# Block-sorted attention with a gated FFN: value mixing of batches 1 to 3 by pairs of 64-row matmuls

## The chip, the cores and the metric

The kernel runs on one core of a Trainium2 chip. The metric is the device time of one execution in microseconds (us). Before the change it was 250.72 us, the median of 5 runs (250.2 to 250.99).

## What is computed

Four batches of eight heads, each a sequence of 768 positions with 64 channels. Each head's sequence is cut into 8 blocks of 96 positions. A small 8x8 matrix P per head is normalised five times over rows and columns. K and V are then mixed block by block with P (each sorted block is a weighted sum of the 8 blocks), and each query block attends to its own sorted block. The result goes through a gated FFN (512 to 1536 to 512).

```
k_sorted = einsum('bhij,bhjcd->bhicd', P, k_b)
v_sorted = einsum('bhij,bhjcd->bhicd', P, v_b)
scores   = scale * q_b @ k_sb^T            # per block of 96
attn     = softmax(scores)
x        = (attn @ v_sb), heads side by side   # 3072 x 512
out      = (silu(x @ w_gate) * (x @ w_val)) @ w_out
```

## The kernel before, in words

**Layout.** There are 64 pairs of (head, block) per batch. V of a batch is loaded with these pairs on 64 partitions: batch 0 and batch 2 on partitions 0 to 63 (`lowr`), batch 1 and batch 3 on 64 to 127 (`highr`). `copy_v` then turns it, for each partition, from (position, channel) order into (channel, position) order in the tile `vch`, so that the 96 positions of one channel lie together. There is one `vch`; batches 0, 1 and the pair of 2 and 3 use it in turn.

**Mixing of the values.** For one channel, a matmul takes the 64 partitions' 96 positions as its stationary operand and a 64x64 matrix `rmix` (P of the eight heads along the diagonal) as its moving operand. Batch 0 does this with 64 rows. For batch 1 all 128 rows of `vch` are multiplied with a `rmix[1]` whose lower 64 rows are zero (`v_chunk`, 64 moving columns). For batches 2 and 3, `rmix["p"]` is 128 x 128, block diagonal over the two batches, so that one matmul per channel gives both (`v_pair_chunk`, 128 moving columns). A chunk fills a PSUM tile of two banks, tag "a" or "b", which ScalarE or VectorE drains into the tile `vt` (`drain`, 96x1024). Batch 1 has four chunks of 16 channels, the pair eight chunks of 8.

**Other matmuls.** `kq_chunk` mixes K and moves Q (output tile tkq); each pair of its matmuls goes to the two column halves of the array. `scores` (qk) runs 64-row matmuls of 96 columns in pairs on the two row halves. `av` applies the softmax. `gate` (g_ps), `value` (v_ps) and `outp` (o_ps) are the FFN, in eight stages of 384 positions.

**Order.** TensorE's and GpSimd's instruction orders are written out by hand. `merge` takes the FFN matmuls of a stage as its main list and slips the attention's pieces in at given positions; batch 1's value chunks lie in stage 1 and the pair's in stage 3. VectorE's and ScalarE's orders are by hand in the start-up and otherwise left to a scheduler. The GpSimd queue issues the loads and the larger casts and does most of `copy_v`: for batch 1 four copies of 64x1536, then the loads `kp` and V of batches 2 and 3 (which reuse V's tile), the casts of Q, and the copies of the pair.

**Weights.** P reaches the 64-partition layout by small matmuls; `w_sb` keeps what the later batches need, in a ScalarE copy for each half of the partitions, and `mix_of` multiplies it with a mask into `rmix` on VectorE.

Of the kernel before, what the change touches and what calls it, by code (L numbers as in the profile page):

```python
# [10 lines left out]
BF16 = mybir.dt.bfloat16  # L11
# [6 lines left out]
def kernel(  # L18
# [11 lines left out]
    nc = tc.nc  # L30

    B, H, S, D = q.shape
    NB = sort_net.shape[-1]
    C = S // NB
# [9 lines left out]
    R = H * NB  # L44
# [9 lines left out]
    const = ctx.enter_context(tc.tile_pool(name="const", bufs=1))  # L54
# [20 lines left out]
    vch = const.tile([128, D * C + 32], BF16)  # L75
    nc.vector.memset(vch[:, D * C:], 0.0)
    vch3 = vch[:, 0:D * C].rearrange("p (d c) -> p d c", c=C)
# [36 lines left out]
        load_w(wg_sb, wg_dram, lo, hi)  # L114
        load_w(wv_sb, wv_dram, lo, hi)

    def copy_v(eng, pair, rows, s, n=4, d0=0, d1=D):
        cs = slice(s * (C // n), (s + 1) * (C // n))
        dst = vch3[rows, d0:d1, cs]
        src = v_tiles[pair][rows, cs, d0:d1]  # L120
        if eng is nc.scalar:
            eng.copy(dst, src.transpose([0, 2, 1]))
        else:
            eng.tensor_copy(dst, src.transpose([0, 2, 1]))  # L124

    ident = const.tile([128, 128], BF16)
    lowr, highr = slice(0, R), slice(R, 2 * R)
# [23 lines left out]
    load_q(1, 0, C)  # L151
    nc.gpsimd.dma_start(out=wo_sb, in_=wo_dram)

    rmix = {b: const.tile([128, 2, H, NB], BF16, name=f"rmix{b}") for b in (0, 1, "p")}
    for t in rmix.values():
        nc.vector.memset(t, 0.0)
# [3 lines left out]
    def vt_tile(pair):  # L160
        if pair not in vts:
            t = vtp.tile([C, 2, H * NB, D + 1], BF16, name=f"vt{pair}", tag="vt")
            nc.vector.memset(t[:, :, :, D:D + 1].rearrange("p u n e -> p (u n) e"), 1.0)
            vts[pair] = t
        return vts[pair]
# [10 lines left out]
    def pair_tile(name, tag):  # L176
        return psum.tile([128, 1024], FP32, name=name, tag=tag)

    def bank_tile(name, tag="gen"):
        return psum.tile([128, 512], FP32, name=name, tag=tag, bufs=3 if tag == "gen" else 1)  # L180
# [28 lines left out]
    def drain(eng, dst, src):  # L209
        if eng == "v":  # L210
            nc.vector.tensor_copy(dst, src)  # L211
        else:
            nc.scalar.copy(dst, src)  # L213
# [10 lines left out]
    def chunk_tile(name, n, tag):  # L224
        return pair_tile(name, tag) if n == 2 else bank_tile(name, tag)
# [10 lines left out]
        drain(eng, dst[:, :, at:at + n], tp.transpose([0, 2, 1]))  # L236

    def v_chunk(b, at, n, eng, tag):
        rows = slice(0, 128) if b % 2 else lowr
        dst = vt_tile(b // 2)[:, b % 2]  # L240
        mix = rmix[b][rows, 0].rearrange("p a b -> p (a b)")
        tp = chunk_tile("tv", n // 8, tag).rearrange("p (l n) -> p l n", n=H * NB)
        for ld in range(n):
            col = (at + ld) * C
            nc.tensor.matmul(tp[:, ld, :], lhsT=vch[rows, col:col + 128], rhs=mix,  # L245
                             start=True, stop=True)
        drain(eng, dst[:, :, at:at + n], tp[0:C].transpose([0, 2, 1]))

    def v_pair_chunk(pair, at, n, eng, tag):
        dst = vt_tile(pair).rearrange("p u n e -> p (u n) e")  # L250
        mix = rmix["p"].rearrange("p u a b -> p (u a b)")
        tp = chunk_tile("tv", n // 4, tag).rearrange("p (l n) -> p l n", n=2 * H * NB)
        for ld in range(n):
            col = (at + ld) * C
            nc.tensor.matmul(tp[:, ld, :], lhsT=vch[:, col:col + 128], rhs=mix,  # L255
                             start=True, stop=True)
        drain(eng, dst[:, :, at:at + n], tp[0:C].transpose([0, 2, 1]))

    es, sts, xts = {}, {}, {}
    ecount = [0]  # L260
# [21 lines left out]
    def exps(b, u, wide, pss):  # L282
        n = ecount[0] % 8
        ecount[0] += 2
        if wide is None:
            for two in range(2):
                nc.scalar.activation(e_all[:, n + two, 0:4 * C], pss[two][0:C, 0:4 * C], AF.Exp, scale=scale)
        else:
            nc.scalar.activation(e_all[:, n:n + 2, 0:4 * C], wide[0:C, :, 0:4 * C], AF.Exp, scale=scale)  # L289
        es[(b, u)] = [e_all[:, n, :], e_all[:, n + 1, :]]  # L290

    def qk(b, u, tag="b"):
        exps(b, u, *scores(b, u, tag))
# [29 lines left out]
    def xtr(b, u):  # L323
        half, g = divmod(u, H2)
        if g == 0:
            xts[(b, half)] = xtp.tile([128, H2, TW], BF16, name=f"xt{b}_{half}", tag="xt")
        x_ps = xt_tile("x", 1)[:, 0]
        x_to(x_ps, b, u)
        return xts[(b, half)][:, g, :], x_ps.rearrange("p a b -> p (a b)")
# [83 lines left out]
    def fill(tile, n):  # L413
        for _ in range(n):
            nc.tensor.matmul(tile, lhsT=warm_sb[:, 0:128], rhs=warm_sb, start=True, stop=True)  # L415
# [7 lines left out]
    for it, n in ((1, 3), (2, 4), (3, 4), (4, 4)):  # L423
        nc.tensor.matmul(idle_ps[0:NB, 0:NB], lhsT=rowreds[it][:, :, 0], rhs=rowreds[it][:, :, 0],
                         start=True, stop=True)
        fill(idle_ps, n)

    def weights(half):
        w_ps = bank_tile(f"w_ps{half}")[:, 0:NB * B * H].rearrange("p (i b h) -> p i b h", b=B, h=H)
        for i in range(NB):  # L430
            nc.tensor.matmul(w_ps[half * R:(half + 1) * R, i].rearrange("p b h -> p (b h)"),
                             lhsT=p_bf[:, i].rearrange("p a b -> p (a b)"),
                             rhs=ident[0:BH, 0:BH], start=True, stop=True)
        return w_ps

    def mix_of(dst, b, w):
        lo = (b % 2) * R
        nc.vector.tensor_tensor(dst, mask[lo:lo + R].unsqueeze(2).to_broadcast([R, H, NB]),
                                w[lo:lo + R].transpose([0, 2, 1]), op=ALU.mult)

    w_lo = weights(0)
    mix_of(rmix[0][lowr, 0], 0, w_lo[:, :, 0])
    w_hi = weights(1)
    w_sb = const.tile([128, NB, 2, H], FP32)
    nc.scalar.copy(w_sb[lowr, :, 1], w_lo[lowr, :, 2])
    nc.scalar.copy(w_sb[highr], w_hi[highr].rearrange("p i (pair u) h -> p i pair u h", u=2)[:, :, :, 1])
    fill(idle_ps, 1)
    v_chunk(0, 0, 8, "v", "gen")
# [15 lines left out]
    for b in range(1, B):  # L464
        rows = highr if b % 2 else lowr
        mix_of(rmix["p"][rows, b % 2] if b > 1 else rmix[1][rows, 0], b, w_sb[:, :, b // 2])
    fill(idle_ps, 4)
    qk(0, 0, "a")
    qk(0, 1, "b")
# [48 lines left out]
    def units(b, us, ats):  # L518
        us = list(us)
        todo = []  # L520
        for n, at in enumerate(ats):
            u, u2 = us[2 * n:2 * n + 2]
            held = []
            todo.append((at, lambda u=u, u2=u2, held=held: (qk(b, u, "b"), held.append(scores(b, u2, "a")))))
            todo.append((at + 1.3, lambda u2=u2, held=held: exps(b, u2, *held[0])))
            for w, tag, t in ((u, "b", 1.9), (u2, "a", 3.6)):
                if b == 0 or b == 1 and u < H2:
                    todo.append((at + t, lambda w=w, tag=tag: av(b, w, tag)))
                    todo.append((at + t + 3.1, lambda w=w: drain("v", *xtr(b, w))))
                else:  # L530
                    todo.append((at + t, lambda w=w, tag=tag: (av(b, w, tag), x_dma(b, w))))
        return todo

    def kqs(b, ats):
        return [(at, lambda n=n: (kq_chunk(b, n * 32, 16, "v", "b"), kq_chunk(b, n * 32 + 16, 16, "s", "a")))
                for n, at in enumerate(ats)]

    def vs(f, size, ats):
        return [(at, lambda m=m: f(1, m * size, size, "sv"[m % 2], "ba"[m % 2])) for m, at in enumerate(ats)]

    def merge(main, side):
        done, k = 0.0, 0
        side = sorted(side, key=lambda t: t[0])
        for c, f in main:
            f()
            done += c
            while k < len(side) and side[k][0] <= done:
                side[k][1]()
                k += 1
        while k < len(side):  # L550
            side[k][1]()
            k += 1

    def ffn(n):
        todo = []
        for m in range(NFC):
            if n > 0 or m > 1:
                todo.append((0.65, lambda m=m: gate(n, m)))
            if n > 0 or m > 0:
                todo.append((0.65, lambda m=m: value(n, m)))  # L560
            ends = (6, 9, 11) if n == 1 else (3, 7, 11)
            if n > 0 and m in ends:
                for part in range(3):
                    todo.append((0.87, lambda t3=ends.index(m), part=part: outp(n - 1, t3, part)))
        return todo

    for s in range(4):
        copy_v(nc.gpsimd, 0, highr, s)
    load_k_pair()
    load_v(2, 0, C)  # L570
    load_v(3, 0, C)
# [1 line left out]
    q_cast(3)  # L573
    both = slice(0, 128)
    merge(ffn(0), units(0, range(4, 8), (0.0, 5.6)))
    merge(ffn(1), vs(v_chunk, 16, (3.2, 3.9, 4.7, 5.5)) + kqs(1, (6.2, 8.2, 10.3)) + units(1, range(4), (11.3, 15.8)))
    for s in range(4):
        copy_v(nc.gpsimd, 1, both, s)
    nc.vector.memset(kqt_tile("p")[:, 2 * GI * C:], 0.0)
# [42 lines left out]
```

The softmax here doesn't subtract the row's maximum and nothing guards it: scores larger than these inputs give would overflow.

## Time and profile before

| | |
|---|---|
| median of 5 runs | 250.72 us |
| the profiled execution, its own time | 250.2 us |
| its span in the profile | 248.2 us |
| PE busy | 239.9 us (97%) |
| DVE, ACT, POOL busy | 157.7, 110.2, 52.6 us |
| batch 1's value matmuls (L245, 128 rows) | 64, in 4 blocks from 47.63 us |
| the pair's value matmuls (L255) | 64, in 8 blocks from 107.75 us |
| score matmuls (L276) | 256, 64 rows |

PE is TensorE's matmuls and PEld its weight loads, DVE VectorE, ACT ScalarE, POOL GpSimd. A matmul's duration in the profile is a latency of about 200 ns; matmuls overlap, so the cost of a block is read from the start of one block to the start of the next. A timeline line gives the start and the length from the first start to the last end. In the chain of waits, pieces are put end to end and so show what each adds. A shape such as 64*128 64x96 is rows*columns of the array that are used and the moving operand.

### The profile page before, as it was taken

Reading aid. Unit: us, or ns where it says so; the run is one execution under the profiler, and the core shown is the slowest. Engines: PE = TensorE matmul, PEld = TensorE weight load, DVE = VectorE, ACT = ScalarE, POOL = GpSimd, SP = SyncE. Lnnn points to the kernel's source line nnn. Section 1 sums busy time; section 2 is a strip of 40 time slices with the busy share of each in tenths; the row PEclk is TensorE's granted clock in tenths of the full one; section 3 lists DMA queues with packets and bytes.
Section 4 is the critical chain, followed back from the end, with each engine's and each line's share of the span. In section 5 each row is a group of like instructions: output and inputs, shape, how many; then the busy total and the mean of one; then the engine's idle time right before and its main releaser. Section 6 shows DMA issues by size and latency. Waiting matters only on the chain.

```text
span 248.2 us, 6062 instructions
## 1 busy us (share of the span) xinstructions
PE 239.9 (97%) x2572; PEld 142.8 (58%) x2572; DVE 157.7 (64%) x332; ACT 110.2 (44%) x187; POOL 52.6 (21%) x47
## 2 busy tenths in 40 slices
PE   7799999999999999999999999999999999999995
PEld 5376566666555556666655655565555555555543
DVE  6777689887555775857657647755764585446700
ACT  2977543453544444455642552354244334232311
POOL 7938449980059200000000000000000000000000
PEclk9999999999999999999999999999999999999999
DMA  5949999999999388110122121112111111100122
GB/s 100 209 84 161 214 192 220 199 223 217 220 171 189 71 186 149 43 42 3 42 51 57 51 68 32 44 45 74 26 52 42 38 56 56 45 18 25 45 81 89
DMA packets 39530, 24.38 MB, mean 98 GB/s; under 512 B 27728, under 2 KB 35664, under 8 KB 38992
## 3 DMA queue, kind: packets, MB, share of 16 engines
q0 software_dynamic: 21328, 14.16, 39.0%
q1 hardware_dynamic: 18176, 9.84, 14.3%
q8 instruction: 20, 0.33, 0.6%
q14 instruction: 6, 0.05, 0.1%
HBM read 28.32 MB, written 7.86 MB: 146 GB/s over the span
## 4 chain that ended last, share of the span: by engine, by line
PE 88%; DVE 6%; ACT 3%; issue 2%; DVEq 0%; ACTq 0%
PE v_ps L372 24%; PE g_ps L354 23%; PE o_ps L389 23%; PE tkq L233 4%; PE av_ps L303 3%; PE qk L276 3%; PE idle_ps L415 2%; PE tv L245 2%; PE tv L255 1%; DVE gs_sb L364 1%; PE o_ps L405 1%; DVE st L309 1%; PE x_ps L320 1%; DVE h L377 1%; ACT e_all L289 1%
## 5 line engine op out<-in xcount | busy, mean ns | idle before, releaser
L364 DVE SCALAR_TENSOR_TENSOR gs_sb<-th_sb,g_ps 128x384 bf16<-128x384 bf16 x96 | 52.8, 550 | 53.8 <-ACT th_sb L362 51.2
L372 PE MATMUL v_ps<-xt,wv_sb 128*128 128x384 bf16 x380 | 77.3, 326 | 0.3
L354 PE MATMUL g_ps<-xt,wg_sb 128*128 128x384 bf16 x376 | 76.5, 325 | 0.0
L362 ACT ACTIVATE th_sb<-g_ps 128x384 bf16<-128x384 f32 x96 | 47.1, 490 | 57.7 <-PE g_ps L354 55.2
L389 PE MATMUL o_ps<-wo_sb,h 128*128 128x512 bf16 x276 | 64.3, 379 | 0.0
L377 DVE SCALAR_TENSOR_TENSOR h<-v_ps,gs_sb 128x384 bf16<-128x384 f32 x96 | 53.3, 556 | 6.4
L372 PEld LDWEIGHTS <-wv_sb 128*128 128x128 bf16 x380 | 35.6, 97 | 23.9 <-issue 1.4
L354 PEld LDWEIGHTS <-wg_sb 128*128 128x128 bf16 x376 | 34.5, 97 | 22.9 <-issue 0.2
L389 PEld LDWEIGHTS <-h 128*128 128x128 bf16 x276 | 26.3, 98 | 28.3
L394 ACT COPY o_sb<-o_ps 128x512 f32<-128x512 f32 x23 | 13.5, 585 | 49.1 <-PE o_ps L389 49.1
L124 POOL COPY vch<-v 64x1536 bf16<-64x1536 bf16 (+2 forms) x11 | 28.7, 2643 | 19.6 <-DMA v<-in_v_dram 19.6
L289 ACT ACTIVATE e_all<-qk 96x768 bf16<-96x768 f32 x30 | 22.6, 802 | 7.7 <-PE qk L276 7.6
L309 DVE TENSOR_TENSOR st<-av_ps,r_sb 96x512 bf16<-96x512 f32 x32 | 21.7, 679 | 0.2
L303 PEld LDWEIGHTS <-e_all 96*128 96x128 bf16 x256 | 12.2, 98 | 5.0 <-ACT e_all L289 0.8
L303 PE MATMUL av_ps<-vt,e_all 96*128 96x65 bf16 x256 | 13.5, 194 | 0.0
L307 DVE RECIPROCAL r_sb<-av_ps 96x8 f32<-96x8 f32 x32 | 6.4, 199 | 8.6 <-PE av_ps L303 8.6
L213 ACT CAST vt<-tv 96x1024 bf16<-96x1024 f32 (+1 forms) x9 | 9.2, 1031 | 3.8 <-PE tv L255 2.6
L211 DVE CAST vt<-tv 96x1024 bf16<-96x1024 f32 (+1 forms) x9 | 9.8, 1100 | 1.1 <-PE tv L245 1.1
L211 DVE CAST kqt<-tkq 128x1024 bf16<-128x1024 f32 (+1 forms) x7 | 7.5, 1068 | 2.6 <-PE tkq L233 2.5
L213 ACT CAST kqt<-tkq 128x1024 bf16<-128x1024 f32 (+1 forms) x7 | 6.0, 894 | 6.5 <-PE tkq L233 6.5
L233 PE MATMUL tkq<-rmix,kq 128*64 128x64 bf16 x384 | 7.8, 197 | 0.5 <-issue 0.5
L233 PEld LDWEIGHTS <-kq 128*64 128x64 bf16 x384 | 6.8, 112 | 2.4 <-issue 2.1
(74 smaller groups left out, 131.9 us busy)
## 6 DMA issues: line engine op xcount, KB each, us to landing
out_dram<-o_sb SPq DMA_DIRECT2D x23, 256.0 KB, 2.0
v<-in_v_dram POOLq DMA_DIRECT2D x3, 768.0 KB, 18.6
kq<-in_q_dram POOLq DMA_DIRECT2D x2, 768.0 KB, 13.5
wg_sb<-in_moe_w_gate_dram POOLq DMA_DIRECT2D x6, 256.0 KB, 8.6
wv_sb<-in_moe_w_val_dram POOLq DMA_DIRECT2D x6, 256.0 KB, 9.6
wo_sb<-in_moe_w_out_dram POOLq DMA_DIRECT2D x1, 1536.0 KB, 24.3
kp<-in_k_dram POOLq DMA_DIRECT2D x2, 768.0 KB, 14.0
q_scr<-in_q_dram POOLq DMA_DIRECT2D x2, 768.0 KB, 28.8
```

Of the source, the lines that this page charges most:

```text
L124: eng.tensor_copy(dst, src.transpose([0, 2, 1]))
L211: nc.vector.tensor_copy(dst, src)
L233: nc.tensor.matmul(tp[two * D:(two + 1) * D, lc, :], lhsT=kq_tiles[b][:, at + lc, :], rhs=rm[:, two], start=True, stop=True)
L289: nc.scalar.activation(e_all[:, n:n + 2, 0:4 * C], wide[0:C, :, 0:4 * C], AF.Exp, scale=scale)
L303: nc.tensor.matmul(o[:, two, i4, :], lhsT=e[:, i4 * C:i4 * C + 128], rhs=vt[:, 2 * g + two, half * 4 + i4, :], start=True, stop=True)
L309: nc.vector.tensor_tensor(st.rearrange("p i two d -> p two i d"), o[0:C, :, :, 0:D], r_sb.to_broadcast([C, 2, 4, D]), op=ALU.mult)
L354: nc.tensor.matmul(g_ps, lhsT=wg_sb[:, kc, ts(m, 128)], rhs=xt[:, kc, :], start=(kc == 0), stop=(kc == NKC - 1))
L362: nc.scalar.activation(th_sb, g_ps, AF.Tanh, scale=0.5)
L364: nc.vector.scalar_tensor_tensor(gs_sb, th_sb, 1.0, g_ps, op0=ALU.add, op1=ALU.mult)
L372: nc.tensor.matmul(v_ps, lhsT=wv_sb[:, kc, ts(m, 128)], rhs=xt[:, kc, :], start=(kc == 0), stop=(kc == NKC - 1))
L377: nc.vector.scalar_tensor_tensor(h_tiles[n][:, m, :], v_ps, 0.5, gs_tiles.pop(m), op0=ALU.mult, op1=ALU.mult)
L389: nc.tensor.matmul(o_ps, lhsT=h_w[:, m, ts(t3, 128)], rhs=wo_sb[:, m, :], start=(m == 0), stop=(m == NFC - 1))
```

## The change

Values of batches 1 to 3 are mixed by 64-row matmuls of 64 columns, two for each step of the loop, one on each row half of the array and each into its own PSUM bank (`v_rows_chunk`). For the pair, the two are batch 2 and batch 3 of the same channel. For batch 1, whose V lies on the upper partitions alone, channels 0 to 31 are copied to the lower partitions and channels 32 to 63 to the upper ones; one matmul takes channel d and the other channel d + 32. GpSimd's copies for this are eight of 64x768 instead of four of 64x1536, and four of them write to other partitions than they read. A copy of batch 1's mixing matrix for the lower rows (`vmix`) is made from a part of `w_sb` that a widened ScalarE copy fills. Chunk counts, drains per chunk and their places in the order stay.

```diff
-    def copy_v(eng, pair, rows, s, n=4, d0=0, d1=D):
+    def copy_v(eng, pair, rows, s, n=4, d0=0, d1=D, to=None):
...
-        dst = vch3[rows, d0:d1, cs]
+        dst = vch3[rows if to is None else to, d0:d1, cs]
...
+    vmix = const.tile([R, H, NB], BF16)
...
+    def v_rows_chunk(mixes, dst, at, step, eng, tag):
+        n = 512 // (H * NB)
+        tp = pair_tile("tv", tag).rearrange("p (w l n) -> p w l n", w=2, n=H * NB)
+        for ld in range(n):
+            for w, rows in enumerate((lowr, highr)):
+                col = (w * step + at + ld) * C
+                nc.tensor.matmul(tp[:, w, ld, :], lhsT=vch[rows, col:col + 128], rhs=mixes[w],
+                                 start=True, stop=True)
+        drain(eng, dst[:, :, :, at:at + n], tp[0:C].transpose([0, 1, 3, 2]))
+
+    def v_one_chunk(b, at, n, eng, tag):
+        dst = vt_tile(b // 2)[:, b % 2, :, 0:D].rearrange("p n (w d) -> p w n d", w=2)
+        mixes = [vmix.rearrange("p a b -> p (a b)"), rmix[b][highr, 0].rearrange("p a b -> p (a b)")]
+        v_rows_chunk(mixes, dst, at // 2, D // 2, eng, tag)
+
     def v_pair_chunk(pair, at, n, eng, tag):
-        dst = vt_tile(pair).rearrange("p u n e -> p (u n) e")
-        mix = rmix["p"].rearrange("p u a b -> p (u a b)")
-        tp = chunk_tile("tv", n // 4, tag).rearrange("p (l n) -> p l n", n=2 * H * NB)
-        for ld in range(n):
-            col = (at + ld) * C
-            nc.tensor.matmul(tp[:, ld, :], lhsT=vch[:, col:col + 128], rhs=mix,
-                             start=True, stop=True)
-        drain(eng, dst[:, :, at:at + n], tp[0:C].transpose([0, 2, 1]))
+        mixes = [rmix["p"][rows, u].rearrange("p a b -> p (a b)") for u, rows in enumerate((lowr, highr))]
+        v_rows_chunk(mixes, vt_tile(pair), at, 0, eng, tag)
...
-    nc.scalar.copy(w_sb[lowr, :, 1], w_lo[lowr, :, 2])
+    nc.scalar.copy(w_sb[lowr], w_lo[lowr, :, 1:3])
...
+    mix_of(vmix, 0, w_sb[:, :, 0])
...
     for s in range(4):
-        copy_v(nc.gpsimd, 0, highr, s)
+        copy_v(nc.gpsimd, 0, highr, s, d0=D // 2)
+        copy_v(nc.gpsimd, 0, highr, s, d1=D // 2, to=lowr)
...
-    merge(ffn(1), vs(v_chunk, 16, (3.2, 3.9, 4.7, 5.5)) + kqs(1, (6.2, 8.2, 10.3)) + ...
+    merge(ffn(1), vs(v_one_chunk, 16, (3.2, 3.9, 4.7, 5.5)) + kqs(1, (6.2, 8.2, 10.3)) + ...
```

More of the change, by code (lines that the diff above doesn't have):

```diff
@@ L238, in v_chunk @@
     def v_chunk(b, at, n, eng, tag):
-        rows = slice(0, 128) if b % 2 else lowr
         dst = vt_tile(b // 2)[:, b % 2]
-        mix = rmix[b][rows, 0].rearrange("p a b -> p (a b)")
+        mix = rmix[b][lowr, 0].rearrange("p a b -> p (a b)")
         tp = chunk_tile("tv", n // 8, tag).rearrange("p (l n) -> p l n", n=H * NB)
@@ L244, in v_chunk @@
             col = (at + ld) * C
-            nc.tensor.matmul(tp[:, ld, :], lhsT=vch[rows, col:col + 128], rhs=mix,
+            nc.tensor.matmul(tp[:, ld, :], lhsT=vch[lowr, col:col + 128], rhs=mix,
                              start=True, stop=True)
         drain(eng, dst[:, :, at:at + n], tp[0:C].transpose([0, 2, 1]))
-    def v_pair_chunk(pair, at, n, eng, tag):
-        dst = vt_tile(pair).rearrange("p u n e -> p (u n) e")
-        mix = rmix["p"].rearrange("p u a b -> p (u a b)")
-        tp = chunk_tile("tv", n // 4, tag).rearrange("p (l n) -> p l n", n=2 * H * NB)
-        for ld in range(n):
-            col = (at + ld) * C
-            nc.tensor.matmul(tp[:, ld, :], lhsT=vch[:, col:col + 128], rhs=mix,
-                             start=True, stop=True)
-        drain(eng, dst[:, :, at:at + n], tp[0:C].transpose([0, 2, 1]))
+    def v_rows_chunk(mixes, dst, at, step, eng, tag):
[11 more added lines that the diff above has]
+        v_rows_chunk(mixes, dst, at // 2, D // 2, eng, tag)
+    def v_pair_chunk(pair, at, n, eng, tag):
+        mixes = [rmix["p"][rows, u].rearrange("p a b -> p (a b)") for u, rows in enumerate((lowr, highr))]
+        v_rows_chunk(mixes, vt_tile(pair), at, 0, eng, tag)
     es, sts, xts = {}, {}, {}
@@ L575 @@
     merge(ffn(0), units(0, range(4, 8), (0.0, 5.6)))
-    merge(ffn(1), vs(v_chunk, 16, (3.2, 3.9, 4.7, 5.5)) + kqs(1, (6.2, 8.2, 10.3)) + units(1, range(4), (11.3, 15.8)))
+    merge(ffn(1), vs(v_one_chunk, 16, (3.2, 3.9, 4.7, 5.5)) + kqs(1, (6.2, 8.2, 10.3)) + units(1, range(4), (11.3, 15.8)))
     for s in range(4):
```

## The prediction

> **What bounds the kernel now.** I read the page first: the engines' busy shares, then the chain that ended last.
>
> ```profile
> PE 239.9 (97%) x2572; PEld 142.8 (58%) x2572; DVE 157.7 (64%) x332; ACT 110.2 (44%) x187; POOL 52.6 (21%) x47
> PE 88%; DVE 6%; ACT 3%; issue 2%; DVEq 0%; ACTq 0%
> ```
>
> TensorE is busy 97% of the span and is 88% of the chain. So a nanosecond taken from or added to its stream between 27 us and the end moves the end, unless it is swallowed by a wait of PE. Next, the groups of instructions with shapes kept apart: the two matmul groups that the change rewrites, and the scores, which already run as 64-row pairs.
>
> ```profile
> L276 PE MATMUL qk<-kqt 64*128 64x96 bf16 x128 | 4.4, 204 | 0.7 <-DVE st L309 0.6
> L255 PE MATMUL tv<-rmixp,vch 128*128 128x128 bf16 x64 | 4.9, 219 | 0.0
> L245 PE MATMUL tv<-rmix,vch 128*128 128x64 bf16 x64 | 2.5, 193 | 0.0
> ```
>
> The means (193 to 219 ns) are latencies; what counts is the distance from start to start. Third, the chain in order of time, 47 to 55 us, with start, length and count of each piece:
>
> ```profile
> 47.14 0.65 PE g_ps L354 x4
> 47.79 0.47 PE tv L245 x16
> 48.26 0.65 PE v_ps L372 x4
> ...
> 52.91 0.62 PE tkq L233 x32
> 53.53 0.04 issue
> 53.57 0.70 PE tkq L233 x32
> ```
>
> A block of 16 batch-1 matmuls costs the chain 0.47 us. The first half of the tkq block takes 0.62, though a whole undisturbed block (56.44) takes 1.13: some 0.2 us is a wait in its middle. Fourth, the timelines of POOL, DVE and PE:
>
> ```profile
> 36.16 11.22 POOL L124 COPY vch<-v 64x1536 bf16<-64x1536 bf16 x4 [2.84 <-DMA v<-in_v_dram]
> ```
> ```profile
> 52.29 1.22 DVE L211 CAST vt<-tv 96x1024 bf16<-96x1024 f32 x1 [0.48 <-PE tv L245]
> ```
> ```profile
> 47.63 0.63 PE L245 MATMUL tv<-rmix,vch 128*128 128x64 bf16 x16
> ...
> 83.99 1.03 PE L389 MATMUL o_ps<-wo_sb,h 128*128 128x512 bf16 x4
> 84.95 0.51 PE L276 MATMUL qk<-kqt 64*128 64x96 bf16 x16
> 85.40 0.39 PE L389 MATMUL o_ps<-wo_sb,h 128*128 128x512 bf16 x1
> ```
>
> POOL ends its copies of batch 1 at 36.16 + 11.22 = 47.38 us, and PE reads them from 47.63: 0.25 us of room, the tightest place of the change. The last DVE drain of batch 1 starts when its matmuls end (DVE had idled 0.48 us for them) and ends at 52.29 + 1.22 = 53.51; tkq's second half continues at 53.57. That drain is the wait in the tkq block.
>
> **What the Trainium skill says.** TensorEngine Tiling (Array Packing), Tiling Modes: "Changing tiling mode (not just tile) drains the TensorE". The trace agrees. Four o_ps matmuls from 83.99 stream until 84.85 (4 x 215.8 ns start to start), qk starts 0.096 us later and o_ps returns at 85.40: 0.54 us for 8 pairs whose streaming is 8 x 42.5 = 0.34. TensorE: Matmul & The Clock Gate, Part 3 "The mechanism", has matmuls on different row groups overlap, about 4 ns apart; single starts of qk show 3 to 4 ns in a pair. GPSIMD Engine Reference, Instruction dispatch, describes a fixed software cost per POOL instruction; the trace agrees (below). I found no price there for a POOL copy whose output lies on other partitions.
>
> **The change part by part.**
>
> 1. *Batch 1, four blocks.* Now 16 matmuls of 64 columns at 29.2 ns (single starts) = 0.467 us. After: 8 pairs. From the qk blocks in FFN work: 96 ns to enter the mode; first pair 52 ns (50 plus 3 in the tkq block, also of 64 columns); and from the last start to FFN's next 135 ns, of which 42.5 is its own streaming, so 92 ns to leave. A pair of 64 columns I take at 29.2 ns: qk's pairs keep the distance of one unpaired matmul of their width (96/2.4 + 2.5 = 42.5), and one of 64 columns, weight load included, shows 29.2. Block: 96 + 52 + 6 x 29.2 + 3 + 29.2 + 92 = 448 ns, so -18 each, four times: -0.07 us. Bounds for the pair distance: 31.8 (tkq's column pairs) and 42.5 (64 columns no faster than 96), giving blocks of 464 and 529 ns.
>
> 2. *Batches 2 and 3, eight blocks.* Now 8 matmuls of 128 columns at 55.8 ns = 0.447 us. After, the same 448 ns: +0.01 us in all. The saved half of the streaming goes into two mode changes. With both bounds, all twelve blocks are worth -0.06 (taken), +0.13, or +0.91 us. There are 64 more matmuls and loads, none early enough to touch the start-up; a qk block of 32 such instructions shows no gap inside.
>
> 3. *The wait in the tkq block.* From the start of its slot, batch 1's last block now finishes at 437 + 193 = 630 ns (last start plus latency), after at 96 + 230 + 193 = 519. DVE is idle then, so the drain ends 0.11 us sooner in the slot, while PE arrives only 0.02 sooner: -0.09 us. Bounds: -0.09 and 0.
>
> 4. *POOL's copies.* Four copies of 64x1536 become eight of 64x768, half written to the other 64 partitions. Single POOL copies: 1536 elements 2.84 us, the 64x288 one 0.66, so 1.75 ns an element and 0.155 fixed: 1.50 us for 768. Consecutive starts overlap by 0.05: 1.446. End: 36.16 + 7 x 1.446 + 1.50 = 47.78. Four of the eight carry a semaphore wait that is long satisfied (for start-up's TensorE, ScalarE and POOL work on vch); at start-up a copy with such a wait came 0.04 later than one without: +0.16, so 47.94. PE's first load waits for it. A DVE result reached a waiting PE matmul after 0.055 us, so PE starts at about 48.00 instead of 47.63 + 0.096 = 47.72: +0.27 us. PE is in order, so the whole FFN stream stands behind that load. Bounds: 0, if the fixed part is nearly nothing (end near 47.2); +0.4, if it is the 0.183 us of the one-element copy (landed) and waits cost more. The crossing of partitions has no row; its bounds are none and a doubling, in the rivals. Below nothing: excluded, since PE doesn't wait for POOL now.
>
> 5. *Behind those copies on POOL*: two kp loads, two v loads, two q casts, 0.56 us later. The last four copies begin at 71.18 behind the v loads and end at 82.4, and PE reads them at 107.75: 25 us of cover. kp is read at 93.08; the q transposes on SP come no earlier, and SP's order is unchanged. Zero; were the cover gone, 0.56.
>
> 6. *Small edits*. The copy of w_sb grows to 64x128 (0.26 us as its twin, was 0.20): +0.06 on ACT, which then idles 0.29 for PE. vmix adds one 0.26 us product on DVE at 20.8, where DVE idles 1.04 until av. Batch 1's ACT drains get runs of 8 (1.19 us as for batches 2 and 3, was 1.06); the tile is wanted 1.1 us after the first ends, and 0.6 after the second. Zero; uncovered, each costs its 0.06, 0.26 or 0.13.
>
> Sum: -0.06 - 0.09 + 0.27 = +0.12 us on the profiled execution's 250.2 (span 248.2 plus 2.0 around it), so 250.3. That execution stands 0.5 under the median of 250.72, to which I add: **250.8 us**. A measurement of this kernel tells about 0.2%, 0.5 us, from no change; this is inside.
>
> **Rivals.**
>
> - *POOL becomes the bound at 47.6 us (slower).* From an end of 47.67 on, PE waits nanosecond for nanosecond. Net +0.5 needs POOL's end near 48.3, that is crossing copies about 0.1 us (6%) slower than in-place ones. Doubled ones, 4 x 1.45, end at 53.7: +5.9 us, 256.6. For: nothing in the trace crosses partitions on POOL. Against: the in-place copies of 64 and of 128 partitions take the same 2.84 us, so the work goes by elements, and those don't change. A few tenths, 251.4, are likelier than the doubling.
> - *The pairs don't pair, or not at 29 ns (slower).* At 42.5, 251.8. With no overlap, 16 x 29.2 + 188 + 23 = 678 ns a block: 4 x 0.21 + 8 x 0.23 = 2.7 us, 253.6. Against: every qk block overlaps, in the same mode.
> - *The mode change is cheaper here (faster).* If half of the 188 ns hides, 12 x 0.094 = 1.1 us, 249.7. For: nothing but that these blocks are shorter. Against: 96 in and 135 out stand in nearly every qk block, whatever FFN group is beside it.
>
> **How the numbers follow.** Forecast, within 0.5 us: 0.64. POOL 0.16 and pairing 0.08 make slower, with 0.02 for unseen waits: 0.26. Cheaper modes 0.07, with 0.03 for waits that shrink: faster 0.10. The range: down to 250.0 (blocks at 448, POOL hidden, a low draw), up to 251.7 (POOL late by tenths, or pairs near 42.5); the doubling and the unpaired case stay out.
>
> **What would show it.** PE blocks of 0.44 to 0.47 us, two starts 3 ns apart; POOL's copies at 1.45 to 1.5 us and the last ending at 47.8 to 48.0; a PE idle of 0.2 to 0.3 us at 47.7 released by POOL; the drain wait in tkq halved. A crossing copy well over 1.6 us, a pair distance over 35 ns, or mode gaps other than 96 and 92 ns would prove a step wrong.

## The result, and the profile after

Median after: 250.68 us (43 runs, 250.13 to 252.2); before, measured beside it: 250.27 us (80 runs, 249.63 to 252.37). The ratio after to before is 1.0015, 95% interval [1.0005, 1.0024], so the change costs 0.37 us (0.13 to 0.60), within the 0.5 us that the prediction can't tell from no change. Ratios leave out runs in which the core was disturbed and medians don't, so below the two can differ a little. The profiled execution after took 250.33 us (before 250.2), its span 248.5 (before 248.2).

The page after begins with the span and the engines' busy times; its section on the chain gives shares by engine.

```profile
span 248.5 us, 6197 instructions
...
PE 240.3 (97%) x2636; PEld 140.0 (56%) x2636; DVE 158.0 (64%) x333; ACT 110.5 (44%) x187; POOL 53.4 (21%) x51
...
PE 74%; DMA 10%; POOL 8%; DVE 3%; issue 2%; ACT 1%; POOLq 0%; DVEq 0%
```

There are 64 more matmuls, and TensorE is as busy as before. New in the chain are POOL with 8% and DMA with 10%: the chain that ended last now runs through POOL's copies and the load that they wait for. Where it does so is seen in the chain in order of time (start, length, piece):

```profile
44.62 1.52 POOL vch L124
46.13 0.05 issue
46.18 1.51 POOL vch L124
47.70 0.05 issue
47.74 0.41 PE tv L255 x16
48.15 0.76 PE v_ps L381 x4
48.91 0.34 PE tv L255 x16
49.24 0.76 PE g_ps L363 x4
50.00 0.65 PE v_ps L381 x4
...
52.84 1.26 PE tkq L234 x64
```

TensorE's first batch-1 pair waits for the last copy. A mode change here is TensorE's going over from matmuls on the full array to matmuls on 64 rows, or back. The idle is 0.13 us, from 47.61, where the FFN stream has ended and the mode change is over (last FFN start plus 258 ns, as at blocks without a wait), to 47.74. A block of pairs shows as 0.34 (the first, behind the wait, as 0.41), and the FFN piece behind it as 0.76 where one with no block ahead of it has 0.65: 0.34 + 0.11 = 0.45 us for a block, against 0.47 before. The same chain in the middle of batches 2 and 3:

```profile
107.10 0.65 PE g_ps L363 x4
107.75 0.34 PE tv L255 x16
108.09 0.76 PE v_ps L381 x4
108.84 0.34 PE tv L255 x16
109.19 0.76 PE g_ps L363 x4
```

Again 0.45 us a block, where the old blocks of 8 matmuls had 0.447. Batches 2 and 3 gained nothing. POOL's and DVE's timelines after:

```profile
35.32 12.36 POOL L124 COPY vch<-v 64x768 bf16<-64x768 bf16 x8 [2.21 <-DMA v<-in_v_dram]
```
```profile
52.13 1.23 DVE L212 CAST vt<-tv 96x1024 bf16<-96x1024 f32 x1 [0.35 <-PE tv L255]
```

The copies take 12.36 us from the first start to the last end, 1.14 more than the four large ones. V happened to land earlier in this execution (copies from 35.32, before from 36.16), which hides most of it. DVE's last drain of batch 1 now ends at 53.36 instead of 53.51, and the tkq block that waits for it is 0.10 us shorter (1132 instead of 1233 ns from its first matmul's start to its last one's).

The copies themselves, by groups with shapes kept apart (busy, mean ns | idle before):

```profile
L124 POOL COPY vch<-v 64x768 bf16<-64x768 bf16 x8 | 12.1, 1507 | 2.5 <-DMA v<-in_v_dram 2.2
```

One copy lasts 1.51 us, whether it stays on its partitions or crosses. Eight would need 8 x 1.51 - 7 x 0.05 = 11.7 us with the overlap of 0.05 us that consecutive copies have before. They took 12.36. Where the other 0.6 us comes from was the first question.

One more difference lies behind the last matmul, where POOL's queue closes the program. Its four semaphore instructions there, before and after (shortest, median and longest in ns, then the first and the last start):

```profile
L617 POOLq EVENT_SEMAPHORE  x4: 17/17/17, 247.4 to 248.1; - x4
```
```profile
L628 POOLq EVENT_SEMAPHORE  x4: 17/17/17, 247.3 to 248.4; - x4
```

By single starts they are 1.15 us from the first to the last, instead of 0.62: POOL stands still for 0.41 us among them. From the last matmul's end to the end of the span the trace after has 3.63 us and the one before 3.09.

### The profile page after: what moved, and what is told of

It reads as the page before. It is cut to its first block, busy times and chain, and to the rows that moved or that the text cites. A ratio compares the mean times of both kernels' runs of the same rounds, so it can differ in the third digit from the quotient of the medians.

```text
span 248.5 us, 6197 instructions
## 1 busy us (share of the span) xinstructions
PE 240.3 (97%) x2636; PEld 140.0 (56%) x2636; DVE 158.0 (64%) x333; ACT 110.5 (44%) x187; POOL 53.4 (21%) x51
## 4 chain that ended last, share of the span: by engine, by line
PE 74%; DMA 10%; POOL 8%; DVE 3%; issue 2%; ACT 1%; POOLq 0%; DVEq 0%
PE o_ps L398 23%; PE v_ps L381 21%; PE g_ps L363 20%; DMA v<-in_v_dram 5%; DMA kq<-in_k_dram 5%; POOL vch L124 4%; PE tkq L234 3%; PE av_ps L312 2%; PE qk L285 2%; PE tv L255 2%; POOL wg_sb L111 1%; POOL wv_sb L111 1%; PE o_ps L414 1%; DVE st L318 1%; DVE gs_sb L373 1%
## 5 line engine op out<-in xcount | busy, mean ns | idle before, releaser
L124 POOL COPY vch<-v 64x768 bf16<-64x768 bf16 (+3 forms) x15 | 29.5, 1986 | 19.5 <-DMA v<-in_v_dram 19.2
L424 PE MATMUL idle_ps<-warm_sb 128*128 128x512 bf16 x28 | 8.5, 400 | 0.0
```

## The experiments

Two explanations of the long copies were tried against each other: it is their **number**, each small copy losing the overlap, or it is the **alternation** of the output between the upper and the lower partitions. Beside these, the pairs were tried without the copies, and versions were built that should give back the time. Whole runs scatter by 2 us (in the one such trace that was kept, e12 below, from loads that land late in stage 0), so a few tenths are read from the stages of the traces.

**e1_pairs_2_3**: the pairs for batches 2 and 3 alone; batch 1 and its copies as before.

```diff
-        copy_v(nc.gpsimd, 0, highr, s, d0=D // 2)
-        copy_v(nc.gpsimd, 0, highr, s, d1=D // 2, to=lowr)
+        copy_v(nc.gpsimd, 0, highr, s)
...
-    merge(ffn(1), vs(v_one_chunk, ...
+    merge(ffn(1), vs(v_chunk, ...
```

> The new matmul pairs for batches 2 and 3 alone; batch 1 keeps its 128-row matmuls and its four in-place copies. My theory: the pairs are a small gain on PE and POOL's longer copies eat it. Then eight blocks at 0.436 us (as in the trace of after) instead of 0.447 give -0.09 us and nothing waits: 250.2 against 250.27, ratio about 0.9997. Rival: the mode changes themselves cost what is missing (colder weight loads, FFN matmuls slower behind a block): then this is slower than before by 0.2 us or more.

Measured: 250.19 us against 250.15, ratio 0.9999 [0.9977, 1.0022]. From the first score matmul of batch 1 to that of batch 2 this trace has 58.861 us, the trace after 58.864 and the one before 58.865: the gain of 0.09 from shorter blocks isn't there. The single starts show why. FFN's stream end to its next start is 435.5 ns over a pair block, 11 less than over an old one, but FFN's second matmul starts 173 ns after its first instead of 162, behind each mode change: 446.5. This execution also showed the old four copies late:

```profile
47.30 0.65 PE g_ps L364 x4
47.95 0.55 PE tv L246 x16
48.50 0.65 PE v_ps L382 x4
49.15 0.47 PE tv L246 x16
```

V's copies began at 36.59 and ended at 47.80, and the first block took 0.55 us where the second took 0.47. The kernel before stands on the edge of this wait already.

**e2_copies**: the kernel before, with eight copies of 64x768 that all stay on their partitions.

```diff
-        copy_v(nc.gpsimd, 0, highr, s)
+        copy_v(nc.gpsimd, 0, highr, s, d0=D // 2)
+        copy_v(nc.gpsimd, 0, highr, s, d1=D // 2)
```

> The kernel before with only its four copies of batch 1 cut into eight of 64x768, all in place, matmuls untouched. Theory A: each 64x768 copy costs POOL 1.55 us from start to start whatever it writes, so the eight take 12.4 us and not 11.2, and PE waits for them at 47.6 us: +0.1 to +0.95 us by when V of batch 1 lands (36.16 us in the trace of before, 35.32 in that of after), about +0.5. Theory B: consecutive copies overlap by 0.05 us as long as they use the same partitions, and only the alternation of partitions made 1.55: the eight then take 11.7 us and the time is +0.0 to +0.3.

Measured: 250.2 us against 250.15, ratio 0.9976 [0.9955, 0.9996]. POOL's timeline:

```profile
35.63 11.73 POOL L124 COPY vch<-v 64x768 bf16<-64x768 bf16 x8 [2.36 <-DMA v<-in_v_dram]
```

The same eight copies without the crossing take 11.73 us, at 1.44 to 1.47 from start to start. The number costs 0.5 us over four copies, not 1.14. The interval of the ratio lies below 1 although this kernel does no less than the one before, so an interval that misses 1 by less than a tenth of a per cent, that of the change included, is weak evidence by itself.

**e4_ordered**: the change, with the four copies that stay first, then the four that cross.

```diff
     for s in range(4):
         copy_v(nc.gpsimd, 0, highr, s, d0=D // 2)
+    for s in range(4):
         copy_v(nc.gpsimd, 0, highr, s, d1=D // 2, to=lowr)
```

> The changed kernel with the four in-place copies first and the four crossing ones after them. Theory B (alternation costs the overlap): six of seven steps fall from 1.55 to 1.45 us, so first start to last end is about 11.8 us. Theory A (every copy of this size costs 1.55): 12.4 us.

Measured: POOL's timeline, and single starts of 1.44 us apart except 1.555 at the one switch:

```profile
35.76 11.69 POOL L124 COPY vch<-v 64x768 bf16<-64x768 bf16 x8 [2.40 <-DMA v<-in_v_dram]
```

So it is the alternation: the crossing copies follow one another as closely as the others (1.43 to 1.45 us), and a switch between the two partition halves costs about 0.1 us. The change has seven, each at 1.54 to 1.57. Why a switch costs this isn't shown. The run took 250.96 us, a single one, with a wait of 1.1 us in stage 0 that ends at 42.89 (v_ps; the trace puts the matmul's wait down to DVE's gs_sb and that of its weight load to the load of wv) and has no POOL in it, so the time says nothing on the copies.

**e3_two_copies** and **e12_two_copies_again**: the change, with two large copies (64x3072) in place of the eight; the same kernel twice.

```diff
-    for s in range(4):
-        copy_v(nc.gpsimd, 0, highr, s, d0=D // 2)
-        copy_v(nc.gpsimd, 0, highr, s, d1=D // 2, to=lowr)
+    copy_v(nc.gpsimd, 0, highr, 0, n=1, d0=D // 2)
+    copy_v(nc.gpsimd, 0, highr, 0, n=1, d1=D // 2, to=lowr)
```

> The changed kernel with batch 1 copied by two instructions of 64x3072 (one in place, one crossing) instead of eight. At 1.75 ns an element and 0.155 us fixed, 5.5 us each, 11.1 together: POOL ends 1.3 us earlier than in the changed kernel, 0.1 earlier than in the one before, and PE no longer waits. If POOL's copies hid the gain of the pairs, this shows it: 12 blocks (-0.21 us) and the shorter drain wait (-0.10) make -0.31 us against before, 249.96, ratio 0.9988. If the loss lies in the mode changes, it stays at 250.6.

> The two-copy kernel a second time, on the chip of the grouped ones, so that what the grouping adds is read on one chip: -0.31 us against before (0.9988), and 0.8 us more than the run with the grouped blocks of batches 2 and 3.

Measured: e3 249.82 us, ratio 0.9986 [0.9967, 1.0004]; e12 250.53 us, ratio 1.0000 [0.9976, 1.0024]. In e3 the copies took 11.04 us (35.07 to 46.11), and the first block had no wait (95 ns to enter the mode). So the wait for POOL is gone, but that is a few tenths, which these intervals don't resolve. e12's profiled execution, 252.68 us, shows what scatters them; PE's timeline:

```profile
38.86 0.82 PE L363 MATMUL g_ps<-xt,wg_sb 128*128 128x384 bf16 x4 [0.94 <-DMA wg_sb<-in_moe_w_gate_dram]
...
44.78 0.82 PE L381 MATMUL v_ps<-xt,wv_sb 128*128 128x384 bf16 x4 [1.20 <-DMA wv_sb<-in_moe_w_val_dram]
```

TensorE waited in stage 0 for weights (2.8 us in the sum of waits), before any matmul that the change touches.

**e7_v_early** and **e8_v_late**: the change, with batch 1's V load issued one step of the weight loads earlier (e7) or later (e8).

```diff
-    for m in range(0, 1024, 256):
+    for m in range(0, 768, 256):      # e7;  e8: range(0, 1280, 256)
         load_gv(m, m + 256)
     load_v(1, 0, C)
-    for m in range(1024, DF, 256):
+    for m in range(768, DF, 256):     # e7;  e8: range(1280, DF, 256)
```

> The changed kernel with the load of batch 1's V issued one step (two weight loads) earlier. If POOL's wait for that load sets the start of its copies and through them PE's stall, the copies start about 1.5 us earlier (34 us), end near 46.5, and PE doesn't wait: -0.3 us against before, ratio 0.9988, like the two-copy run. Rival: the displaced weight loads hold up stage 0 of the FFN by as much: no gain.

> The changed kernel with that load issued one step later. By the same reasoning the copies start about 1.3 us later (36.6 to 37.5), end at 49 to 49.9, and PE idles at its first pair block for the difference to 47.6: 1.4 to 2.3 us, and the time rises by as much: 252 to 253.

Measured: e7 250.55 us, ratio 1.0003 [0.9980, 1.0027], a miss. POOL's timeline:

```profile
33.46 0.53 POOL L102 DMA_DIRECT2D kq<-in_q_dram  x1 [3.40 <-DMA v<-in_v_dram]
34.51 1.04 POOL L152 DMA_DIRECT2D wo_sb<-in_moe_w_out_dram  x1 [0.51 <-DMA wg_sb<-in_moe_w_gate_dram]
35.60 12.34 POOL L124 COPY vch<-v 64x768 bf16<-64x768 bf16 x8
```

The copies no longer wait for V, but POOL itself comes to them as late: it issues wo's load at 34.51, in the trace after at 32.07, since the loads ahead of it waited. The landing and POOL's own queue lie side by side here, and moving one uncovers the other. In this trace TensorE doesn't wait for POOL all the same: it waited 0.5 us for loads of wv first, which the trace after doesn't show, and came to its first block at 48.13, when the copies had ended at 47.94. So the rival in the expectation, weights that come later, is what this trace shows.

e8 took 254.43 us (one run). The waits from 47 to 56 us of its trace:

```profile
PE tv L255 <- POOL vch L124: 2.2, 1, 2.2
```

The copies ran from 38.06 to 50.40, and TensorE's first block started at 50.45, so the 2.2 us arrived there in full. The kernel lost more than that. Windows of the stretches behind the wait (sum of time; busy time of PE, PEld, DVE, ACT, POOL; granted clock; DMA share; GB/s):

```profile
50.00:52.00 2.00, 1.55 (x36) 1.05 (x36) 0.34 (x1) 1.10 (x1) 2.00 (x5) 0.88 1.24 207
52.00:55.00 3.00, 3.00 (x26) 1.25 (x22) 2.11 (x4) 0.58 (x2) 3.00 (x3) 0.51 1.28 235
```

From about 1 us after the idle, at 51.5, to 54.9 us the clock was granted at half: four g_ps matmuls took 1.46 us instead of 0.82. That is about 1.5 us more. TensorE had also come to the block 0.6 us later than in the trace after (48.22 against 47.61), and its wait is 2.1 us longer than that trace's 0.13. Together this is 4.2 us, where the run stands 4.1 above that one (254.43 against 250.33). No other trace has so long an idle or half the clock between its first FFN matmul and its last; the two were seen together once.

**e5_group_2_3**, **e9_two_group**: the eight blocks of batches 2 and 3 put two by two behind one another (e5), which saves four mode changes; e9 adds e3's two copies.

```diff
-    merge(ffn(3), vs(v_pair_chunk, 8, [1.15 * n for n in range(8)]) + ...
+    merge(ffn(3), vs(v_pair_chunk, 8, [2.3 * (n // 2) for n in range(8)]) + ...
```

> The changed kernel with the eight pair blocks of batches 2 and 3 run two by two, back to back, so that four mode changes in and four out fall away. My theory: a block is 96 ns in, 217 of pairs, 93 out and its last pair; a double one is then 0.436 + 8 x 0.0292 = 0.669 us instead of 0.871: four times -0.20, -0.8 us against the changed kernel, 249.9 (ratio to before about 0.998). Rival: the lost time is not a mode change but the 64-row blocks themselves, or the drains of two blocks at once hold PE up: -0.2 us or less.

> The changed kernel with batch 1 copied by two POOL instructions and only the blocks of batches 2 and 3 run two by two; stage 1 keeps its order. If both savings stand and add: -0.31 - 0.81 = -1.1 us against before (ratio 0.9956), all of the second part after 107 us, where no load is under way. If the grouped blocks lose something that the block times do not show (drains, later waits), it stays near the two-copy kernel's -0.3.

Measured: e5 250.28 us, ratio 0.9988 [0.9966, 1.0010]; e9 249.63 us, ratio 0.9979 [0.9955, 1.0002]. Both gain about half of what was expected. In e5 a double block takes 669 ns, as expected, so four mode changes save about 0.8 us; the stage saves 0.45. PE's timeline shows the rest:

```profile
112.54 0.81 PE L363 MATMUL g_ps<-xt,wg_sb 128*128 128x384 bf16 x4
113.57 0.81 PE L381 MATMUL v_ps<-xt,wv_sb 128*128 128x384 bf16 x4 [0.21 <-DVE gs_sb L373]
```

and DVE's why:

```profile
111.84 1.21 DVE L212 CAST vt<-tv 96x1024 bf16<-96x1024 f32 x1
112.98 0.54 DVE L373 SCALAR_TENSOR_TENSOR gs_sb<-th_sb,g_ps 128x384 bf16<-128x384 bf16 x1
```

With two blocks at once DVE has a drain of 1.21 us ahead of gs_sb, for which v_ps waits: by the single starts v_ps is 0.38 us late. A part of each saved mode change becomes this wait. In e5 the copies (35.65, 12.38 us) also ended at 48.03, and PE waited 0.61 us for them, until 48.09, nearly five times what the trace after shows.

**e6_group_all**, **e11_group_again**, **e10_out_later**: e9, with batch 1's blocks two by two as well (e6; e11 is the same kernel); e10 moves three output blocks of that stage later besides.

```diff
-    merge(ffn(1), vs(v_one_chunk, 16, (3.2, 3.9, 4.7, 5.5)) + kqs(1, (6.2, 8.2, 10.3)) + ...
+    merge(ffn(1), vs(v_one_chunk, 16, (3.9, 3.9, 5.8, 5.8)) + kqs(1, (7.1, 8.2, 10.3)) + ...
...
-            ends = (6, 9, 11) if n == 1 else (3, 7, 11)
+            ends = (8, 10, 11) if n == 1 else (3, 7, 11)   # e10 only
```

> Both cures together: all twelve blocks run two by two (batch 1's at 3.9 and 5.8 of stage 1, the first tkq block 0.65 us later), and batch 1 copied by two POOL instructions. Theory: -0.31 us (pairs without the POOL wait) and 6 x -0.20 us (mode changes) against the kernel before, 248.7 of 250.2, ratio 0.994. Rival: drains of two blocks at once make tkq or the second double block wait, and half of it is lost: 0.997.

> The kernel with all twelve blocks grouped and two copies, a second time, for a narrower interval and another profile. By the theory that wo's load takes the gain back, a profile near the median shows PE waiting at its first output matmul; by the start-up theory it shows the same blocks, and the loss before 47 us.

> The kernel with all twelve blocks grouped and two copies, and in stage 1 the first output matmuls moved two steps of the hidden dimension later (8, 10, 11 in place of 6, 9, 11). Theory: in the grouped kernel TensorE comes to its first output matmul at 56.6 us, when the load of wo (issued at 31.6 to 32.3, 24 us) lands at 55.4 to 56.6, so that in many runs the gain ends in a wait for that load. Moved 2.6 us later there is none: -1.4 us against before, ratio 0.9945, with less spread. Rival: the spread comes from the start-up or from the loads before; then it is as the grouped kernel, 0.9975.

Measured: e6 249.88 us, ratio 0.9975 [0.9952, 0.9997]; e11 249.91 us, ratio 0.9991 [0.9967, 1.0016]; e10 248.79 us (14 runs), ratio 0.9939 [0.9901, 0.9978]. e6 and e11, the same kernel, gain far less than the expected 1.5 us. e10 is 1.35 us under before's 250.14 measured beside it, and below the kernels before and after. From FFN's first matmul to the last one its trace has 218.72 us, before 219.90 and after 219.84. Why e10 beats e6 and e11 isn't shown: that the output matmuls had been waiting for wo was a guess, and e11's trace has no such wait. All three hold a gap in the third tkq block; PE's timeline of e10:

```profile
58.72 0.91 PE L234 MATMUL tkq<-rmix,kq 128*64 128x64 bf16 x45
60.50 0.48 PE L234 MATMUL tkq<-rmix,kq 128*64 128x64 bf16 x19 [0.87 <-issue]
```

After the 45th of 64 matmuls TensorE stands for 0.87 us with no engine or load to wait for; in e11 for 0.44, in e6 for 0.13. The record has a lead. The traces hold the transfers of the DMA queue q8, which the page calls instruction, 16 KB each. The last one ahead of this place starts at 57.97 us in e10, 58.29 in e11 and 57.16 in e6, and TensorE goes on 2.53, 2.33 and 2.29 us after that start. In the eleven other traces it comes to this place 2.6 us or more after it, and there is no gap. So TensorE seems to wait for its own instructions here; no run tested it.

## Why the prediction was right, and where a term was off

The forecast of 250.8 us stands 0.1 above the median, and the forecast of +0.12 us beside a measured +0.37 (0.13 to 0.60). That the level fits so well is luck in part: it was built on 250.72, the median of 5 runs, 0.45 above the 250.27 of 80 runs, and that made up for a loss that was put 0.25 too low.

1. *Batch 1's blocks*, -0.07: held. A block is 446.5 ns (448 predicted), so 4 x 0.020 = -0.08. The parts were off and cancelled: the first pair takes 39 ns instead of 52 (-13), and FFN's second matmul comes 11 ns late, which the prediction didn't have. Its bounds of 464 and 529 ns left the block's last pair at 29.2 ns; by its own sum they are 466 and 541, so +0.15 and +1.05 us for all twelve, which no run came near. Entering (96 ns), the pair distance (29.2) and the 3 ns inside a pair held, so "the pairs don't pair" falls.
2. *Batches 2 and 3*, +0.01: held; 58.864 against 58.865 us over that stretch. Halved streaming and two mode changes cancel exactly, as the trace after and e1 show. The Trainium skill says that a change of tiling mode drains TensorE (TensorEngine Tiling (Array Packing), Tiling Modes); the traces agree, with 96 ns in, 93 out and 11 behind. "The mode change is cheaper here" falls.
3. *The wait in the tkq block*, -0.09: held, -0.10.
4. *POOL's copies*, +0.27: the mechanism held, the size didn't. The step has 11.78 us from the first start to the last end. With copies that stay it is 11.73 (e2); in the change it is 12.36. The term that was mis-sized is the distance of 1.446: it took the overlap of 0.05 from copies whose output lies on the same partitions, and where the output alternates the distance is 1.55. Seven switches of some 0.09 us each are the missing 0.63. Crossing itself, for which the prediction had no measured price and which it named as the danger, costs nothing, 1.51 us both ways; but the rival "POOL becomes the bound" asked for 0.1 us more on four copies, and 0.1 on seven switches is that and more.
   The second thing the step lacked is that the start isn't fixed. Over the eleven traces with V's load in its old place and no such delay as in e12 the copies begin between 34.80 and 36.59. With 12.36 us of copies and PE ready at 47.61, the wait grows one for one with a start later than 35.2: 0.13 us in the trace after, 0.61 in e5 (where PE was ready a little earlier), and by this sum some 1.0 had it begun at 36.16 as in the trace before. PE's own arrival isn't fixed either: in the eight of these traces that keep the first block in its place PE could have begun it between 46.97 (e3) and 48.41 us (e4). An estimate that puts copies of 12.36 us behind each of these eight starts, and takes PE's own arrival in each, gives waits of 0 to 1.1 us, 0.5 in the mean. None of this was measured run by run.
5. *POOL's later work*, and 6. *the small edits*, zero: held. From batch 1's first value matmul to the last matmul of the kernel the trace after has 196.89 us and the one before 197.18. Of these 0.29 us 0.10 only move ahead of the first matmul, where the mode change now lies; the other 0.19 are steps 1 to 3 (0.08 + 0.10), so nothing else was won or lost on that way.
7. *The end of the program* has no term in the prediction, and it changed. The six traces with eight copies (after, e2, e4, e5, e7, e8) have 3.48 to 3.63 us behind their last matmul, the eight with four or two copies 3.09 to 3.12. In all six POOL stands still for 0.40 to 0.43 us behind its 68th instruction, waiting and closing ones counted; in the other eight it has only 65 or 66. Since e2 has it without a pair or a crossing, it goes with the number of copies. A part comes back outside the span: the time of a run exceeds its span by 1.78 us in the mean of the runs after, by 2.05 in those of before. So about 0.54 - 0.27 = 0.27 us of the loss lies here. Why POOL pauses isn't shown, and no run took the end apart.

So the result is a gain of 0.2 us on TensorE, and two losses that both come from eight copies on POOL: a wait at the first block and a longer end. With 0.27 us for the end, the wait's mean is by subtraction 0.37 + 0.18 - 0.27 = 0.28 us, with an uncertainty as wide as the measured interval; the estimate of 0.5 lies at its upper edge. How the loss divides between the two is not measured. The forecast of the change fell close because gain and loss were each small, and because the start of 36.16 that it took was a late one (the eleven have a mean of 35.54), which made up for copies counted 0.58 us too short.

## What to carry to other kernels

Cost a 64-row block among full-array work with its two mode changes, here 0.2 us in all: eight pairs of 64 columns only break even with eight matmuls of 128, and it is blocks put together that gain (669 ns for two, e5). Before cutting a helper engine's work into more pieces, take its margin over several executions, not one: a load that landed anywhere within 1.8 us decided here, by the estimate above, whether 1.1 us of extra copying cost 0 or 1 us. Look also behind the last matmul, where instructions added to a helper's queue cost about 0.27 us here. And when mode changes are saved by grouping, look at the engine that drains the blocks, since two drains in a row delay what is queued behind them (0.38 us in e5).

## What the runs showed of the hardware that wasn't expected

- POOL's copies overlap by 0.05 us when one follows another on the same output partitions; on a switch between the halves they are 0.04 us apart instead (1.55 against 1.43 to 1.47 us from start to start). To copy 64x768 across partitions costs nothing (1.51 us both ways).
- The second full-array matmul behind a 64-row block starts 11 ns late (173 ns against 162 for 384 columns, 227 against 216 for 512).
- After 2.2 us without a matmul, TensorE's granted clock was 0.51 between 52 and 55 us (e8, one run), so the idle cost nearly twice its length. Waits of 0.1 us (after) to 1.2 us (e12) showed nothing of the kind.
- Eight copies in place of four or two go with a pause of 0.40 to 0.43 us on POOL's queue behind the last matmul, in six traces of six.
- The gap of 0.13 to 0.87 us after the 45th matmul of a tkq block (e6, e11, e10) appears, in fourteen traces, only where TensorE comes there within 2 us of the start of a 16 KB transfer of instructions, and ends 2.3 to 2.5 us after that start. That it is a wait for them is likely, not tested.
